# One block of a small transformer on one core: five q/k tiles in place of six, x loaded ahead of the weights, the first v product in three parts, and all engines' orders anew

## The chip, the cores and the metric

One Trainium2 chip, one core of it. The time is that of one execution of the whole kernel on the device, in microseconds (us); a kernel is compared by the median of several runs. The core has five engines that run their own instruction streams and wait for one another by semaphores: PE multiplies matrices, DVE and ACT do vector work and move results out of PE's accumulators (PSUM), POOL does small vector work, and SP issues the DMA transfers.

## The reference, cut to what matters

```python
x = A_x                                    # 2048 tokens x 448, bf16
h = x + A(layernorm(x), wqkv, wo)          # attention
out = h + B(layernorm(h), w_in, w_sp, b_sp, w_out)
# A: 16 heads of 28; token t sees t, t-2, ..., t-14; softmax over those 8; then @ wo
# B: z = gelu(h_n @ w_in); z1, z2 = halves of 896; z2 = layernorm(z2)
#    g = w_sp (2048x2048) @ z2 + b_sp; out = (z1 * g) @ w_out
```

## The kernel before, in words

Everything stays in on-chip memory; x is 16 blocks of 128 tokens. The work goes in these steps.

1. **Load.** SP issues 14 loads: x (16 blocks, in pieces of 1, 1, 2, 4, 4, 4), the q and k columns of `wqkv` (three parts into `wraw`, here wq_0, wq_1, wq_2 with 224, 448 and 224 KB), the v columns (two parts into `wv`, 224 KB each) and `wo` (three parts).
2. **Normalise.** For each block DVE takes statistics (L616, L618), POOL the inverse deviation (L610, L611), and DVE writes the normalised block `xn` (L627). Blocks 0 to 3 are transposed by PE (job xT, L656) and copied out of PSUM into `xhT` (job xe); blocks 4 to 15 are transposed by DMAs of SP.
3. **Weights.** DVE and ACT copy `wraw` into `wqk` with heads padded to 32 columns: jobs wp0 to wp3, k = 0 and 1 (336 columns each, need wq_0 and wq_1), and wp4_0, wp4_1 (448 columns, need wq_2).
4. **q and k.** For each tile of tokens in `QT` and each group of four heads one product of eight matmuls (L691 to L709): six full-height ones, "F", and two half-height ones, "H", that run side by side. Before there are six tiles, of 128, 128, 256 and three times 512 tokens. Job qk1_3H is the H part of tile 1, group 3; job qe evacuates the two PSUM banks into `qkT` on ACT or DVE. For tile 0 (`NF2 = 1`) the F part is two jobs, F0 and F1, that wait apart.
5. **v.** One product (job v0, v2, ..., v16, L715 to L731) for two of 18 attention blocks; six F and two H matmuls of 448 columns; job ve evacuates into `V1`.
6. **Attention.** For each block b: logits (jobs lg, two of 8 narrow matmuls each), exp on ACT (ex), mask on DVE (mk), E times V on PE (o), reciprocal and division on DVE (rc, om), a transposing DMA (oT). Then the output projection (y), residual and second layernorm.
7. **MLP.** Products with `w_in` (z1, z2), gelu on ACT, then 28 long products with `w_sp` (L950, job g) and the last ones with `w_out` (L974, job wo), residual add on DVE (L981, job r) and the store of each block.

The order on every engine isn't worked out when the kernel is built: `ORDER` lists all jobs by number in one sequence, each engine takes its own in that sequence, and `BANK` gives each product its PSUM banks. `ON` says which engine makes each evacuation or copy. A job waits for the jobs whose data or PSUM bank it needs; what stands behind it on the same engine waits with it. One filler job, "warm" (L989), is a matmul on constant data that may be listed many times; it stands there 32 times, 31 of them ahead of the first q and k product and one among the first ones.

Of the kernel before, what the change touches and what calls it, by code (L numbers as in the profile page):

```python
# [6 lines left out]
D = 448  # L7
# [6 lines left out]
NK = 128  # L14
# [11 lines left out]
ORDER = [1, 114, 23, 28, 5, 930, 930, 29, 4, 930, 930, 24, 930, 2, 930, 930, 3, 37, 25, 930, 39, 930, 6, 930, 930, 40, 930, 9,  # L26
# [41 lines left out]
BANK = [2, 1, 4, 5, 4, 6, 6, 0, 2, 0, 4, 2, 6, 0, 4, 6, 2, 4, 6, 2, 0, 4, 2, 0, 4, 2, 0, 0, 0, 2, 6, 1, 2, 0, 0, 2, 6, 4, 1,  # L68
# [9 lines left out]
ON = {'xe0_1': 'dve', 'xe0_0': 'dve', 'wp0_0': 'dve', 'wp2_1': 'dve', 'wp4_0': 'act', 'wp4_1': 'act', 'wp1_1': 'dve',  # L78
# [4 lines left out]
    'act', 've4': 'act', 'qe4_1': 'dve', 'od2': 'pool', 'od3': 'pool', 'qe4_3': 'dve', 've8': 'act', 'od4': 'pool',  # L83
    'qe4_0': 'dve', 'qe4_2': 'act', 've10': 'act', 'od6': 'dve', 'od5': 'pool', 'qe5_3': 'act', 'od7': 'pool', 'od8':
    'dve', 've12': 'act', 've14': 'act', 'qe5_1': 'act', 'qe5_0': 'act', 'od9': 'pool', 'od11': 'pool', 'od10':
    'pool', 'qe5_2': 'act', 'z2c1': 'act', 've16': 'act', 'z2c3': 'act', 'oc11': 'dve', 'z2c2': 'act', 'od12': 'pool',
    'oc12': 'act', 'od13': 'pool', 'z2c4': 'act', 'z2c5': 'act', 'z2c7': 'dve', 'z2c6': 'act', 'oc13': 'dve', 'od14':
    'dve', 'od15': 'pool', 'oc15': 'dve', 'od17': 'dve', 'oc14': 'dve', 'od16': 'pool', 'oc17': 'act', 'oc16': 'act',
    'z2c8': 'act', 'z2c9': 'act', 'z2c13': 'act', 'z2c10': 'act'}
RAW2 = [0, 1, 2, 1, 1, 1, 1, 2, 1, 2, 1, 0, 0, 1, 0, 0]  # L90
XEH = {0: 2}
# [9 lines left out]
FK = [(0, 2, 3), (0, 1, 3)]  # L101
# [218 lines left out]
def bass_sequential_preLN__sliding_local_dilated__mixer_gmlp__prompt_kernel(  # L320
# [17 lines left out]
    with contextlib.ExitStack() as top:  # L338
# [125 lines left out]
        def psv(t, k=0, n=512, p=128):  # L464
            c = (t.b + k) * 512
            return psum[0:p, c:c + n]
# [580 lines left out]
```

## Time and profile before

| | us |
|---|---|
| median of 3 runs | 242.99 (242.45 to 243.13) |
| the profiled execution's own time | 243.36 |
| its span in the trace | 241.6 |
| first q and k product starts on PE | 8.78 |
| the last add on DVE, behind PE's last matmul, starts | 239.08 |
| granted TensorE clock | 0.999 |

A row of a timeline gives the start, the time that the merged instructions took together, the engine, the line, the operation, the tiles, the shape and the count; in brackets the idle time ahead of it and what ended that. A row of the windows gives for one stretch of time the busy time of each engine with its number of instructions, the granted clock, the busy share of the DMA engines and the GB/s that they moved. "SPq" is SP's issuing of a DMA; "PEld" is PE's loading of weights. Some matmul records are missing from a trace: where one is, PE seems idle for the length of one matmul while its weight load is there.

### The profile page before, as it was taken

To read this page: it belongs to the slowest core of one execution; us is meant where nothing else is said; L and a number is where in the kernel's file an instruction comes from. 1 tells how busy PE (TensorE), PEld (TensorE's weight loads), DVE (VectorE), ACT (ScalarE), POOL (GpSimd) and SP (SyncE) were. 2 spreads that over 40 slices of the span, in tenths; PEclk is the share of its full clock that TensorE was granted. 3 is DMA by queue.
4 is the path that set the end of the run, shared out by engine and by line. 5 is a ranking of instruction groups with operands and counts; after the bars stand their busy time and mean duration, and the time that the engine had idled before them with its cause. 6 is when DMAs were issued, how large, how long until landed. Compare 5 with 4: busy or idle time off the path is not lost.

```text
span 241.6 us, 4270 instructions
## 1 busy us (share of the span) xinstructions
PE 234.5 (97%) x1742; PEld 115.9 (48%) x1759; DVE 148.9 (62%) x321; ACT 92.5 (38%) x116; POOL 33.3 (14%) x76
## 2 busy tenths in 40 slices
PE   7899999999999999999999999999999999999995
PEld 5665454554555554444444444444444444444443
DVE  4899987999886988798793143043109232245264
ACT  4687577884898887859440000000000000000000
POOL 6332202003250210131451000000000000000000
PEclk9999999999999999999999999999999999999999
DMA  6943354536749496889999990000000001100112
GB/s 171 341 120 69 65 109 97 133 87 158 164 87 132 90 136 126 174 137 180 188 199 209 187 171 0 3 0 0 0 3 19 19 1 49 49 0 0 38 60 76
DMA packets 66394, 23.23 MB, mean 96 GB/s; under 512 B 58694, under 2 KB 66246, under 8 KB 66374
## 3 DMA queue, kind: packets, MB, share of 16 engines
q1 hardware_dynamic: 66304, 22.95, 45.8%
q8 instruction: 14, 0.23, 0.4%
q14 instruction: 6, 0.05, 0.1%
q10 hardware_dynamic: 70, 0.00, 0.0%
HBM read 6.84 MB, written 1.84 MB: 36 GB/s over the span
## 4 chain that ended last, share of the span: by engine, by line
PE 92%; DVE 2%; DMA 2%; ACT 1%; SPq 1%; issue 1%; DVEq 0%
PE psum L950 40%; PE psum L498 38%; PE psum L974 9%; PE psum L789 3%; PE psum L813 3%; DMA wraw<-in_A_wqkv_dram 2%; DVE st L616 1%; SPq L529 1%; ACT V L514 0%; ACT E L798 0%; DVE wqk L514 0%; DVE xn L627 0%; DVE mv L618 0%; DVE srg L981 0%; DVE qkT L514 0%
## 5 line engine op out<-in xcount | busy, mean ns | idle before, releaser
L959 DVE TENSOR_TENSOR ub<-psum,bb 128x512 bf16<-128x512 f32 x28 | 19.2, 689 | 56.6 <-PE psum L950 56.1
L950 PE MATMUL psum<-wsp_hi,z2p 128*128 128x512 bf16 x219 | 49.9, 379 | 0.3
L798 ACT ACTIVATE E<-psum 128x896 bf16<-128x896 f32 (+2 forms) x36 | 31.7, 932 | 8.2 <-PE psum L789 8.2
L950 PEld LDWEIGHTS psum<-wsp_hi,z2p 128*128 128x128 bf16 x224 | 21.9, 98 | 26.0
L498 PE MATMUL psum<-xhT,wqk 128*128 128x512 bf16 (+5 forms) x186 | 27.3, 307 | 1.5 <-DVE wqk L514 0.5
L950 PE MATMUL psum<-wsp_lb,z2p 128*128 128x512 bf16 x109 | 25.5, 379 | 0.1
L950 PE MATMUL psum<-wsp_la,z2p 128*128 128x512 bf16 x109 | 25.0, 379 | 0.2
L498 PE MATMUL psum<-w_in,hnT 128*128 128x448 bf16 (+1 forms) x128 | 24.6, 353 | 0.0
L498 PE MATMUL psum<-hnT,w_in 128*128 128x512 bf16 (+1 forms) x112 | 23.8, 380 | 0.0
L974 PE MATMUL psum<-w_out,z1p 128*128 128x448 bf16 (+1 forms) x119 | 22.8, 341 | 0.0
L616 DVE BATCH_NORM_STATS2 st<-x_tm 128x6 f32<-128x448 bf16 x32 | 18.8, 612 | 1.8 <-DMA x_tm<-in_A_x_dram 1.7
L804 DVE TENSOR_TENSOR E<-E,maskb 128x1792 bf16<-128x1792 bf16 (+2 forms) x18 | 19.4, 1092 | 0.7 <-ACT E L798 0.7
L876 DVE BATCH_NORM_STATS2 st<-z2p 128x6 f32<-128x448 bf16 x32 | 18.5, 607 | 1.7 <-ACT z2p L872 1.1
L498 PEld LDWEIGHTS psum<-xhT,wqk 128*128 128x128 bf16 (+1 forms) x192 | 12.7, 97 | 12.9 <-issue 4.1
L981 DVE TENSOR_TENSOR srg<-psum,x_tm 128x448 bf16<-128x448 f32 (+1 forms) x17 | 9.9, 594 | 13.3 <-PE psum L974 7.8
L950 PEld LDWEIGHTS psum<-wsp_la,z2p 128*128 128x128 bf16 x112 | 10.9, 98 | 13.2
L950 PEld LDWEIGHTS psum<-wsp_lb,z2p 128*128 128x128 bf16 x112 | 11.0, 98 | 13.2
L611 POOL TENSOR_TENSOR rs<-rs,negh 128x2 f32<-128x2 f32 (+2 forms) x22 | 16.9, 770 | 1.8
L610 POOL TENSOR_SCALAR rs<-mv 128x2 f32<-128x2 f32 (+2 forms) x22 | 7.7, 352 | 66.3 <-DVE mv L618 47.1
L974 PEld LDWEIGHTS psum<-w_out,z1p 128*128 128x128 bf16 x119 | 11.6, 98 | 10.3
L498 PEld LDWEIGHTS psum<-w_in,hnT 128*128 128x128 bf16 (+1 forms) x128 | 10.4, 97 | 11.8 <-issue 3.0
L917 ACT ACTIVATE z1p<-psum 128x1024 bf16<-128x1024 f32 x14 | 14.1, 1021 | 4.5 <-PE psum L498 4.5
(53 smaller groups left out, 228.6 us busy)
## 6 DMA issues: line engine op xcount, KB each, us to landing
w_in<-in_B_w_in_dram SPq DMA_DIRECT2D x8, 224.0 KB, 3.2
out_dram<-srg SPq DMA_DIRECT2D x16, 112.0 KB, 1.8
x_tm<-in_A_x_dram SPq DMA_DIRECT2D x3, 448.0 KB, 7.1
w_out<-in_B_w_out_dram SPq DMA_DIRECT2D x1, 784.0 KB, 5.6
bb<-in_B_b_sp_dram SPq DMA_DIRECT2D x1, 512.0 KB, 5.2
wraw<-in_A_wqkv_dram SPq DMA_DIRECT2D x2, 224.0 KB, 2.9
wraw<-in_A_wqkv_dram SPq DMA_DIRECT2D x1, 448.0 KB, 5.7
wv<-in_A_wqkv_dram SPq DMA_DIRECT2D x2, 224.0 KB, 6.9
```

Source lines behind the costliest of these rows:

```text
L498: ins = e.matmul(o, w, x, start=g not in seen, stop=left[g] == 0, **kw)
L610: [(lambda e: e.tensor_single_scalar(A, mv[:, m:m + n, 1], EPS, ALU.add), r_mv[k][m:m + n], [rr]), (lambda e: e.tensor_tensor(R, A, negh[: ...
L611: (lambda e: e.tensor_tensor(R, A, negh[:, 0:1].to_broadcast([128, n]), ALU.pow), [rr, r_negh], r_rs[k][m:m + n])],
L616: [(lambda e: e.bn_stats(st[:, m, :], src), [rsrc], [r_st[k][m]])], dve_t(D))
L798: return e.activation(o, i, AF.Exp, scale=SCALE)
L804: return e.tensor_tensor(a, a, maskb[:, 0:1, pad:pad + nq].to_broadcast([NK, NHEAD, nq]), ALU.mult)
L876: [(lambda e, m=m, k=k: e.bn_stats(st3[:, m, k, :], z2p[:, m, D * k:D * (k + 1)]), [r_z2[m]], [r_st[2][m]])], dve_t(D))
L917: return e.activation(o, i, AF.Gelu_apprx_tanh)
L950: ins = e.matmul(psv(tk), z2p[:, s, 128 * fc:128 * fc + 128], w[:, 512 * (tc % 2):512 * (tc % 2) + 512], start=(s == 0), stop=(s == NB - 1))
L959: [(lambda e, tc=tc, s=s, tk=tk: e.tensor_tensor(ub[:, s, :], psv(tk), bb[:, 512 * tc:512 * tc + 512], ALU.add), [r_bb], [r_ub[s]])], dve_ ...
L974: ins = e.matmul(psv(tk, 0, c1 - c0), z1p[:, fc, 128 * m:128 * m + 128], w_out[:, fc, c0:c1], start=(fc == 0), stop=(fc == FC7 - 1))
L981: [(lambda e, m=m, s=s, tk=tk, c0=c0, c1=c1: e.tensor_tensor(srg[:, s, c0:c1], psv(tk, 0, c1 - c0), x_tm[:, m, c0:c1], ALU.add), [r_x[m]], ...
```

## The change

- `QT` has five tiles: 256, 256 and three times 512 tokens. So 64 matmuls of 128 columns become 32 of 256, eight evacuations of 256 columns become four of 512, and there are four products and four evacuations less. Tile 0, whose F part is in two jobs, now has 256 tokens and needs blocks 0 and 1 of x.
- `FIRST` and `ORDER` change the order of the loads. Before: x0, x1, wq_2, wq_0, wq_1, x2 (blocks 2 and 3), x4 (4 to 7), x12, wo_1, wv_0, wv_1, x8, wo_2, wo_0. After: x0, x1, x2, x4, wq_1, wq_0, wq_2, x8, wo_1, wv_0, wo_0, x12, wo_2, wv_1.
- The F part of v0 is two jobs, one for each attention block, with waits of their own; each waits for both parts of `wv` and for its own blocks of x. The other v products stay as they are.
- `ORDER`, `BANK` and `ON` are new throughout. PE begins with 22 warm matmuls, xT0, 7 warm, xT1, 3 warm, xT2, xT3, then all eight products of the first two tiles (512 tokens), then v0F0 v0F1 v0H v2H lg3_1 lg0_1 v2F v4F lg1_1 lg0_0 v4H and tile 2 (from qk2_2H on). Before it was xT0 and xT1, the products of the two 128-token tiles, xT2, the logits of block 0, xT3, v0, the 256-token tile with the logits of block 1 among it, v2, the logits of block 2, o1, o0, and then the first 512-token tile (from qk3_3F on). The jobs ve2, ve4 and ve8 go from ACT to DVE, and of the evacuations of 512-token tiles three are on DVE and not five.
- At the end PE did wo12, wo13, wo14 and last the two halves of wo15 (224 columns each); now it does both halves of wo15 first, then wo10, wo13, wo12 and last wo14 (448 columns).

```diff
-FIRST = [(0, 1), "q", (1, 2), (2, 4), "v", (4, 8), (8, 12), (12, 16), "o"]
+FIRST = [(0, 1), (1, 2), "v", "q", (2, 4), (4, 8), (8, 12), (12, 16), "o"]
-QT = [(0, 128), (128, 256), (256, 512), (512, 1024), (1024, 1536), (1536, 2048)]
+QT = [(0, 256), (256, 512), (512, 1024), (1024, 1536), (1536, 2048)]
...
-                load_c("wv", wv, A_wqkv[:, 2 * D:3 * D], D, W_v, 0.9, parts=[(None, 0, 2, 0), (None, 2, 2, 192)])
+                load_c("wv", wv, A_wqkv[:, 2 * D:3 * D], D, W_v, 1.05, parts=[(None, 0, 2, 0), (None, 2, 2, 192)])
...
-                return (
-                    [(i, psv(tk, i, D), xhT[:, c, k0:k0 + NK], wv[:, c, :], None) for i, k0 in enumerate(k0s) for c in FK[i]],
-                    [(i, psv(tk, i, D), xhT[p0:p0 + 64, c, k0:k0 + NK], wv[p0:p0 + 64, c, :], (p0, 0))
-                     for i, (k0, (c, p0)) in enumerate(zip(k0s, HK))])
+                fs = [[(i, psv(tk, i, D), xhT[:, c, k0:k0 + NK], wv[:, c, :], None) for c in FK[i]] for i, k0 in enumerate(k0s)]
+                hs = [(i, psv(tk, i, D), xhT[p0:p0 + 64, c, k0:k0 + NK], wv[p0:p0 + 64, c, :], (p0, 0))
+                      for i, (k0, (c, p0)) in enumerate(zip(k0s, HK))]
+                return fs + [hs] if b == 0 else [sum(fs, []), hs]
...
-            product("v%d" % b, key, f, W_v + xh_res(lo, hi), D, 3 * nb, tk, [o_jobs.get(b + i - NV) for i in range(nb)])
+            rd = W_v + xh_res(lo, hi)
+            if b == 0:
+                rd = [W_v + xh_res(k0, k0 + NK) for k0 in k0s]
+            product("v%d" % b, key, f, rd, D, 3 * nb, tk, [o_jobs.get(b + i - NV) for i in range(nb)], hreads=W_v + xh_res(lo, hi))
```

`ORDER` (962 entries before, 951 after), `BANK` and `ON` are lists of numbers and names, and left out here; what they do to the parts named above is told in the list.

More of the change, by code (lines that the diff above doesn't have):

```diff
@@ L25 @@
 LOOK = {'pe': 0.009410205530073946, 'act': 1e-09, 'dve': 0.19498114580727732, 'pool': 1e-09, 'sp': 0.13408016923274957}
-ORDER = [1, 114, 23, 28, 5, 930, 930, 29, 4, 930, 930, 24, 930, 2, 930, 930, 3, 37, 25, 930, 39, 930, 6, 930, 930, 40, 930, 9,
[41 rows of a table removed]
-BANK = [2, 1, 4, 5, 4, 6, 6, 0, 2, 0, 4, 2, 6, 0, 4, 6, 2, 4, 6, 2, 0, 4, 2, 0, 4, 2, 0, 0, 0, 2, 6, 1, 2, 0, 0, 2, 6, 4, 1,
[4 rows of a table removed]
+ORDER = [1, 27, 23, 25, 38, 2, 919, 28, 919, 8, 919, 29, 919, 919, 9, 37, 919, 24, 919, 6, 919, 114, 39, 919, 919, 5, 919, 40,
[40 rows of a table added]
+BANK = [2, 1, 4, 5, 2, 6, 0, 2, 0, 4, 6, 4, 6, 4, 6, 0, 2, 4, 4, 6, 0, 6, 0, 2, 0, 2, 2, 0, 2, 4, 1, 6, 2, 4, 0, 4, 4, 4, 1,
[4 rows of a table added]
 KEY = dict(x=-10.145, xs=0.685, qk=-3.702, qkg=-1.064, v=-1.761, ve=-6.148, qe=-3.15, lg=-1.488, ex=5.497,
@@ L77 @@
 WINB = 2
-ON = {'xe0_1': 'dve', 'xe0_0': 'dve', 'wp0_0': 'dve', 'wp2_1': 'dve', 'wp4_0': 'act', 'wp4_1': 'act', 'wp1_1': 'dve',
[4 rows of a table removed]
[L83 to L89, printed above, removed]
+ON = {'xe0_0': 'act', 'xe1_0': 'act', 'wp3_0': 'act', 'wp2_0': 'act', 'xe0_1': 'dve', 'wp1_0': 'dve', 'wp2_1': 'dve',
[3 rows of a table added]
+    'act', 'qe3_3': 'dve', 'od0': 'pool', 'od1': 'pool', 'qe2_1': 'act', 've6': 'act', 'qe3_0': 'dve', 'od3': 'pool',
+    'od2': 'pool', 'qe3_2': 'act', 've8': 'dve', 'od4': 'dve', 'od6': 'pool', 'qe3_1': 'act', 'qe4_1': 'act', 'qe4_0':
+    'act', 'od5': 'pool', 'qe4_2': 'act', 'qe4_3': 'act', 've10': 'act', 'od7': 'dve', 'od8': 'dve', 'od9': 'dve',
+    've14': 'act', 've16': 'act', 've12': 'act', 'od11': 'pool', 'od10': 'pool', 'oc11': 'dve', 'z2c1': 'act', 'z2c3':
+    'act', 'z2c2': 'dve', 'od12': 'pool', 'od13': 'pool', 'oc12': 'act', 'oc13': 'act', 'od15': 'dve', 'od14': 'pool',
+    'z2c4': 'act', 'od17': 'pool', 'oc14': 'act', 'oc15': 'act', 'od16': 'dve', 'oc17': 'dve', 'z2c6': 'act', 'z2c7':
+    'act', 'z2c5': 'act', 'oc16': 'dve', 'z2c9': 'act', 'z2c8': 'act', 'z2c10': 'act', 'z2c13': 'act'}
 RAW2 = [0, 1, 2, 1, 1, 1, 1, 2, 1, 2, 1, 0, 0, 1, 0, 0]
```

96 rows, old and new, of tables (BANK, ON, ORDER) are left out of this document.

## The prediction

> **What bounds the kernel now.** I read the page first, then the chain of waits in order of time, then the windows of its stages.
>
> ```profile
> span 241.6 us, 4270 instructions
> ...
> PE 234.5 (97%) x1742; PEld 115.9 (48%) x1759; DVE 148.9 (62%) x321; ACT 92.5 (38%) x116; POOL 33.3 (14%) x76
> ```
>
> ```profile
> 2.67 5.68 DMA wraw<-in_A_wqkv_dram
> ...
> 8.45 0.80 DVE wqk L514 x4
> ...
> 87.20 33.95 PE psum L498 x182
> ...
> 239.08 0.39 DVE srg L981
> ```
>
> ```profile
> core 0: us, PE busy (x) PEld busy (x) DVE busy (x) ACT busy (x) POOL busy (x), PEclk, DMA share, GB/s
> 2.00:8.00 6.00, 5.46 (x37) 4.07 (x36) 3.42 (x8) 2.41 (x5) 3.96 (x13) 1.00 0.90 258
> 8.00:13.00 5.00, 4.52 (x82) 3.61 (x84) 4.55 (x14) 3.91 (x11) 0.95 (x2) 1.00 1.09 366
> 8.78:22.38 13.60, 13.04 (x201) 8.94 (x201) 13.48 (x36) 11.65 (x22) 3.08 (x7) 1.00 0.60 175
> 22.38:87.20 64.82, 63.97 (x765) 32.56 (x772) 57.16 (x116) 50.20 (x59) 13.66 (x26) 1.00 0.56 109
> 87.20:121.20 34.00, 33.95 (x183) 14.70 (x182) 27.96 (x72) 24.88 (x30) 7.80 (x17) 1.00 0.88 162
> 121.20:239.08 117.88, 117.32 (x556) 55.26 (x565) 45.69 (x90) 2.45 (x3) 3.63 (x7) 1.00 0.26 52
> ```
>
> The kernel has three parts. Until 8.78 us it waits for q and k's weights: wq_1 lands at 2.67 + 5.68 = 8.35, the copies into `wqk` begin at 8.45. From 22.38 to 239.08 PE is full (63.97 of 64.82, 33.95 of 34.00, 117.32 of 117.88; most of what is left are missing records). In between, 8.78 to 22.38, PE and DVE are both all but full, and what follows the last matmul is one DVE instruction and a store. So the time is: when PE's first product starts, plus PE's work, plus PE's waits, plus the tail. The change keeps every product after the first 512 tokens; only these four can move.
>
> **Part 1, the start.** These rows give durations and landings.
>
> ```profile
> 1.51 4.55 PE L989 MATMUL psum<-warm 128*128 128x256 bf16 x21 [1.51 <-DVE warm L585]
> ...
> 2.87 0.63 DVE L616 BATCH_NORM_STATS2 st<-x_tm 128x6 f32<-128x448 bf16 x1 [1.42 <-DMA x_tm<-in_A_x_dram]
> 3.15 1.53 SPq L529 DMA_DIRECT2D x_tm<-in_A_x_dram  x3
> ...
> 7.05 1.25 PE L989 MATMUL psum<-warm 128*128 128x256 bf16 x10
> ...
> 8.43 1.23 ACT L514 ACTIVATE wqk<-wraw 128x336 bf16<-128x336 bf16 x3 [0.59 <-DMA wraw<-in_A_wqkv_dram]
> ...
> 9.31 3.39 PE L498 MATMUL psum<-xhT,wqk 128*128 128x128 bf16 x58
> ...
> 10.44 1.65 DVE L616 BATCH_NORM_STATS2 st<-x_tm 128x6 f32<-128x448 bf16 x3
> ...
> 12.54 0.39 PE L656 MATMUL psum<-ident,xn 128*128 128x128 bf16 x4
> 12.85 0.42 PE L789 MATMUL psum<-qkT 28*128 28x128 bf16 x16
> 13.18 0.37 DVE L618 BATCH_NORM_AGGREGATE mv<-st 128x2 f32<-128x6 f32 x4
> 13.77 1.28 DVE L514 CAST xhT<-psum 128x512 bf16<-128x512 f32 x2
> 13.91 1.60 PE L498 MATMUL psum<-wv,xhT 128*128 128x448 bf16 x8 [0.30 <-DVE qkT L514]
> 15.10 0.73 DVE L627 TENSOR_SCALAR xn<-x_tm,mv,rs 128x512 bf16<-128x512 bf16 x2
> 15.35 1.14 PE L498 MATMUL psum<-xhT,wqk 64*128 64x256 bf16 x10
> 15.54 5.22 SPq L528 DMA_TRANSPOSE xhT<-xn  x4
> 18.68 1.57 ACT L514 ACTIVATE qkT<-psum 128x512 bf16<-128x512 f32 x3
> ```
>
> ```profile
> x_tm<-in_A_x_dram SPq DMA_DIRECT2D x1, 224.0 KB, 5.8
> ...
> wo<-in_A_wo_dram SPq DMA_DIRECT2D x1, 336.0 KB, 7.7
> ...
> xhT<-xn SPq DMA_TRANSPOSE x12, 2.5
> ```
>
> Loads land in the order of issue. Up to wq_1 SP had issued 1120 KB, landed at 8.35; the next, x2's 224 KB, issued at 3.15, landed 5.8 later, at 8.95: 0.6 for 224 KB, as the 366 GB/s of the second window say. After the change wq_1 stands behind 896 KB of x, so it is complete with byte 1344 KB, wq_0 with 1568 KB, wq_2 with 1792 KB: 8.95, 9.55, 10.15. The bounds: by 8.00 the engines had moved 6 x 258 = 1548 KB in all, so if all ran level wq_0 lands at 8.1; if the wq parts are as slow behind x as they were in front, 10.2. I take 9.55.
>
> DVE has a chain of its own before the first copy now: six statistics (1.65 / 3 = 0.55), four aggregates (0.1 to 0.18), four normalisations (0.36), one half evacuation (0.4): 5.7 from 2.87, and some 0.7 of waits for x1, x2 and x4 to land, 9.3. Weights and DVE come out together; with 0.1 until the copy starts and 0.3 for it the first product starts at 9.95, not 8.78: **1.17 later**. Bounds 9.5 (DVE) and 10.6 (late weights).
>
> **Part 2, PE from there to the first 512-token tile.** Slots: 0.056 at 128 columns (58 in 3.39, the last with 0.2 of fill), 0.11 at 256 (two side-by-side pairs and six in 1.14), 0.19 at 448 (six and a pair in 1.60 with a change from full to half height, which costs 0.1). A product is seven slots. After: eight products, 56 x 0.11 = 6.2; four changes of height, 0.4; two waits, for wp3_1 and wp4_1 (ACT's copies take 1.23 / 3 = 0.41 each, one after another) and for a bank that qe0_1 frees, 0.2: PE comes to v0 at 16.75. Then v0, v2, v4, 21 x 0.19 = 4.0, four logits jobs at 0.2, five changes, 0.5: 22.05. ACT keeps up (ve0 ends at 19.3, ahead of v4 at 20.0). DVE frees v2's banks at some 22.15; I take 22.15 for the start of tile 2.
>
> ```profile
> 21.27 0.96 PE L813 MATMUL psum<-V,E 128*128 128x29 bf16 x32
> ...
> 22.38 0.99 PEld L498 LDWEIGHTS psum<-xhT,wqk 128*128 128x128 bf16 x6 [0.25 <-issue]
> ```
>
> Before, the same tile began at 22.38. By then PE had also done lg2 (0.4) and o0, o1 (0.9), by 22.15 after the change it has done v4 (1.33) instead: equal. So the opening **gains 0.23**. What pays for the 1.17: xT2 and xT3 are done before the weights come (0.4), the old waits go (13.60 - 13.04 = 0.56 of idle PE, some 0.8 with the fill of matmuls that counts as busy), six changes of height less (0.6), fewer small slots (0.1); less 0.3 of new waits. This list, coarser than the count, leaves 0.4; I keep the count.
>
> Two things sit close. xT4 to xT7 must land by then: after its first weight copy DVE has another, xe2 (0.64), the two wider copies (0.3 each), five statistics, four aggregates and n0_4, 5.0 in all, and so ends n0_4 at 15.2, against 15.10 + 0.4 before; the four transposes take 5.22 of SP and land 2.5 after issue, the last at 21.8 to 22.2. The loads ahead of them on SP are the same fourteen, so it isn't held longer. And v0 waits for wv_1, now the last load; the last load before (wo_0, issued 9.2) landed 7.7 later, at 16.9, against PE's 16.75. A wait of up to 0.3 is possible there; I take 0. The split of v0 by block is worth nothing: both parts wait for the same `wv`, and all of their x is there since xT1.
>
> **Part 3, the middle.** From tile 2 on the same matmuls follow in another order, with one change of height more (0.1). The old order had no wait there. The new one gives DVE three v evacuations and takes two of 512-token q/k tiles away:
>
> ```profile
> L514 ACT ACTIVATE V<-psum 128x896 bf16<-128x896 f32 x9 | 8.2, 920 | 5.4 <-PE psum L498 5.3
> ...
> L514 DVE CAST qkT<-psum 128x1024 bf16<-128x1024 f32 x5 | 6.1, 1216 | 0.4 <-PE psum L498 0.4
> ...
> L514 DVE CAST z2p<-psum 128x896 bf16<-128x896 f32 x1 | 1.1, 1083 | 0.0
> ```
>
> 3 x 1.08 - 2 x 1.22 = 0.8 us more for DVE, which has 57.16 of 64.82 busy. The cover is those 7.6 us; it is thinnest at o1, where DVE between 22.2 and mk1's end has ve4, qe2_2, two masks and small work, about 6.1, and PE about 6.4 of products ahead of o1. I put the middle's waits at 0.2 (from 0 to 1.5).
>
> **Part 4, the tail.** The last group is now 448 wide:
>
> ```profile
> L981 DVE TENSOR_TENSOR srg<-psum,x_tm 128x448 bf16<-128x448 f32 x15 | 9.1, 621 | 13.0 <-PE psum L974 7.5 <-DMA out_dram<-srg 5.5
> ...
> L981 DVE TENSOR_TENSOR srg<-psum,x_tm 128x224 bf16<-128x224 f32 x2 | 0.8, 391 | 0.3 <-PE psum L974 0.3
> ```
>
> 0.62 - 0.39 = **0.23 later**; matmul columns and the store are the same.
>
> **Sum**, against the profiled execution's 243.36: - 0.23 + 0.23 + 0.2 = 243.56. That execution lies 0.37 above the median of the runs, 242.99, so I forecast 243.2 for the median: nearly no change. Its own range is 242.3 to 243.7.
>
> **Rivals.** (a) *DVE takes over in the middle*: if it is more than 0.4 late at mk1, o1 waits, and as PE is full after that, nothing is caught up. With its 0.8 more and a last transpose 0.3 late that is 0.7 at o1 and as much again where ve8 stands ahead of rc6 and om6: 1.2 to 1.4, so 244.3. For it: DVE is busy 13.48 of 13.60 in the opening; against it: the 7.6 idle. (b) *The weights come as if all DMA engines ran level*: start at 9.5, no waits on copies or in the middle: 0.45 + 0.2 + 0.2 less, 242.35; with the waits of xT gone, 242.2. Against it: wq_1 landed at 8.35 although 1548 KB had been moved by 8.00. (c) *PE goes cold before the first product.* The 21 first warm matmuls took 0.21 each, the ten at 7.05 took 0.11: PE begins at half speed and needed some 4 us. After the change only 10 warm and 16 transposing matmuls stand between 6.3 and 9.95. If that is too thin, some 4 us of products run at half speed, 2 us: 245.2. Against it: PE was about as idle from 6.2 to 8.78 (waits of 0.5 and 0.7), and its 58 first products ran at 0.056. The Trainium skill (TensorE: Matmul & The Clock Gate, Part 1: The HAM clock gate) says that the clock is halved again after an idle window of about 3.4 us; no gap here is that long, so by that rule (c) doesn't happen, and the trace agrees as far as its gaps go. (d) *The change does not do what it says* for v0, as told: no time by itself, up to 0.3 if wv_1 is late, inside the forecast.
>
> **Chances.** Forecast with (d) 47%, (a) 31%, (b) 16%, (c) 6%. A measurement of this kernel tells about 0.3% (0.73 us) from no change. So faster 0.17, same 0.47, slower 0.36. Eight times in ten the time lies in 242.2 to 244.7: that takes in (b) and (a) and leaves out (c) and the far ends of the waits.
>
> **What would show it.** Right: the first L498 matmul at 9.5 to 10.6 after wraw's landing, no L656 work after it; tile 2's first weight load near 22.15; windows from there to 121 with under 0.5 us of idle PE beyond missing records; a last L981 of 0.62. Wrong: PE waiting for `wv` or `xhT` DMAs near 17 or 22, rows L813 or L498 with idle time ended by DVE between 25 and 60, matmuls of 256 columns at 0.21 after the start, or a first product before 9.3.

## The result and the profile after

| | before | after |
|---|---|---|
| median of the runs, us | 242.84 (12 runs) | 242.01 (12 runs, 241.32 to 242.84) |
| ratio | 1 | 0.9969 (0.9957 to 0.9981) |
| the profiled execution's own time | 243.36 | 242.38 |
| first q and k product | 8.78 | 9.99 |
| tile 2, first weight load | 22.38 | 21.70 |
| last add on DVE starts | 239.08 | 237.86 |
| its duration | 0.39 | 0.62 |

The kernel became 0.83 us faster (0.3%), where no change was forecast; against the profiled execution the sum said 243.56, and it is 242.38. One execution of a run told below ("after, exchanged and wo15 last") took 479.76 us for a reason that no trace shows; its ratio leaves it out, and the other five lie between 240.44 and 241.14. The page after has the same shares of busy time as before:

```profile
span 240.7 us, 4205 instructions
...
PE 233.6 (97%) x1711; PEld 114.9 (48%) x1727; DVE 148.9 (62%) x319; ACT 93.6 (39%) x115; POOL 32.3 (13%) x75
```

Next the windows, over the stretches that the prediction used:

```profile
core 0: us, PE busy (x) PEld busy (x) DVE busy (x) ACT busy (x) POOL busy (x), PEclk, DMA share, GB/s
...
8.78:22.38 13.60, 12.54 (x127) 8.02 (x128) 12.03 (x38) 10.54 (x19) 3.52 (x8) 1.00 0.62 171
22.38:87.20 64.82, 64.23 (x807) 32.90 (x812) 57.10 (x108) 54.04 (x64) 12.50 (x24) 1.00 0.56 109
87.20:121.20 34.00, 33.95 (x185) 14.77 (x185) 27.94 (x69) 26.10 (x30) 6.60 (x14) 1.00 0.76 137
```

PE is as full from 22.38 on as it was (64.23 of 64.82 against 63.97). In the opening DVE, which had 13.48 of 13.60, now has 12.03. The chain of waits gives the start, and the timeline the way from there to tile 2 (start, length, engine; in brackets the idle time ahead and what ended it):

```profile
3.26 6.37 DMA wraw<-in_A_wqkv_dram
...
9.65 0.29 DVE wqk L512
...
9.99 8.37 PE psum L496 x74
...
237.86 0.62 DVE srg L982
```

```profile
9.65 0.45 DVE L512 COPY wqk<-wraw 128x336 bf16<-128x336 bf16 x2 [0.69 <-DMA wraw<-in_A_wqkv_dram]
...
9.99 6.75 PE L496 MATMUL psum<-xhT,wqk 128*128 128x256 bf16 x64 [0.90 <-DVE wqk L512]
...
16.58 1.78 PE L496 MATMUL psum<-wv,xhT 128*128 128x448 bf16 x10
...
18.29 0.59 PE L790 MATMUL psum<-qkT 28*128 28x112 bf16 x16
...
18.82 2.44 PE L496 MATMUL psum<-wv,xhT 128*128 128x448 bf16 x12
...
20.16 1.09 DVE L512 CAST V<-psum 128x896 bf16<-128x896 f32 x1 [0.30 <-PE psum L496]
...
21.70 0.13 PEld L496 LDWEIGHTS psum<-xhT,wqk 64*128 64x128 bf16 x2
...
22.29 1.24 PE L496 MATMUL psum<-xhT,wqk 128*128 128x512 bf16 x5 [0.16 <-issue]
```

No row of PE between 9.99 and 21.70 has idle time ahead of it: the waits that the prediction put there (0.2 for copies and a bank, 0.1 for DVE) did not come. The landing of q and k's weights still sets the start, as before.

Where the 0.98 us of the profiled execution comes from, by the prediction's own marks: the start is 9.99 - 8.78 = 1.21 later; from there to tile 2 it takes 11.71 and not 13.60, 1.89 less; from tile 2 to the last add 237.86 - 21.70 = 216.16 and not 216.70, 0.54 less; the last add is 0.23 longer. Together 0.99 less.

### The profile page after: what moved, and what is told of

It reads as the page before. It is cut to its first block, busy times and chain, and to the rows that moved or that the text cites. A ratio compares the mean times of both kernels' runs of the same rounds, so it can differ in the third digit from the quotient of the medians.

```text
span 240.7 us, 4205 instructions
## 1 busy us (share of the span) xinstructions
PE 233.6 (97%) x1711; PEld 114.9 (48%) x1727; DVE 148.9 (62%) x319; ACT 93.6 (39%) x115; POOL 32.3 (13%) x75
## 4 chain that ended last, share of the span: by engine, by line
PE 93%; DMA 3%; DVE 1%; SPq 1%; issue 1%
PE psum L496 39%; PE psum L951 39%; PE psum L975 9%; PE psum L814 3%; PE psum L790 3%; DMA wraw<-in_A_wqkv_dram 3%; SPq L527 1%; DVE ub L960 1%; DVE z1p L963 0%; DVE srg L982 0%; DVE wqk L512 0%
## 5 line engine op out<-in xcount | busy, mean ns | idle before, releaser
L496 PE MATMUL psum<-xhT,wqk 128*128 128x512 bf16 (+3 forms) x154 | 26.5, 335 | 1.7 <-DVE wqk L512 0.9
L614 DVE BATCH_NORM_STATS2 st<-x_tm 128x6 f32<-128x448 bf16 x32 | 19.3, 613 | 2.0 <-DMA x_tm<-in_A_x_dram 2.0
L496 PEld LDWEIGHTS psum<-xhT,wqk 128*128 128x128 bf16 (+1 forms) x160 | 12.1, 97 | 11.7 <-issue 2.8
L512 ACT ACTIVATE qkT<-psum 128x1024 bf16<-128x1024 f32 (+1 forms) x17 | 13.6, 825 | 3.3 <-PE psum L496 3.0
L496 PEld LDWEIGHTS psum<-hnT,w_in 128*128 128x128 bf16 (+1 forms) x112 | 8.9, 97 | 12.2 <-issue 2.8
```

The costliest lines, as they stand in the source:

```text
L496: ins = e.matmul(o, w, x, start=g not in seen, stop=left[g] == 0, **kw)
L512: j = pl.job(name, eng, key, [(lambda e: e.activation(o(), i(), AF.Copy) if eng == "act" else e.tensor_copy(o(), i()), list(reads), list(w ...
L614: [(lambda e: e.bn_stats(st[:, m, :], src), [rsrc], [r_st[k][m]])], dve_t(D))
```

## The experiments

Every run is told by its ratio to the kernel before on the same chip (whose medians there were 242.6 to 242.9), and its profiled execution by three stretches. In the expectations P is the theory that time follows PE's own list of work, and T that other engines or waits set it. The mark in the table is the first full-height matmul of tile 2, because every profile shows it; it lies 0.25 after the weight load named above in the kernel before, and 0.59 after it in the changed kernel, which begins tile 2 with a half-height pair.

| kernel | median, ratio | first product | from it to the mark | mark to last add | last add |
|---|---|---|---|---|---|
| before | 242.84, 1 | 8.78 | 13.85 | 216.45 | 0.39 |
| before, loads of x first | 244.18, 1.0052 | 9.53 | 13.78 | 216.45 | 0.39 |
| before, five tiles | 244.84, 1.0076 | 8.24 | 16.45 | 216.45 | 0.39 |
| before, logits jobs exchanged | 242.01, 0.997 | 8.51 | 13.75 | 215.65 | 0.39 |
| after | 242.01, 0.9969 | 9.99 | 12.30 | 215.57 | 0.62 |
| after, once more | 241.5, 0.9948 | 9.64 | 12.31 | 215.75 | 0.62 |
| after, v0 in one piece | 242.1, 0.9969 | 10.23 | 12.31 | 215.51 | 0.62 |
| after, logits jobs exchanged | 240.93, 0.9931 | 9.12 | 12.09 | 215.15 | 0.62 |
| after, wo15 last | 241.64, 0.9968 | 9.81 | 12.39 | 215.54 | 0.39 |
| after, weights ahead of x4 | 241.46, 0.9952 | 8.83 | 12.61 | 215.56 | 0.62 |
| after, exchanged and wo15 last | 241.08, 0.9925 | 9.39 | 12.16 | 215.25 | 0.39 |
| after, all three edits | 241.04, 0.9928 | 8.98 | 12.62 | 215.15 | 0.39 |

### The middle: pairs of logits jobs

From tile 2 on the changed kernel runs nearly the same matmuls in another order and needs 0.54 less. (Ahead of tile 2 it now has v4; behind it, one pair of logits jobs more, o0 and o1.) In the chain of waits, each row of 16 narrow matmuls is two logits jobs next to each other on PE. Before:

```profile
32.41 0.33 PE psum L789 x16
...
34.86 0.50 PE psum L789 x16
...
40.54 0.50 PE psum L789 x16
...
47.71 0.50 PE psum L789 x16
...
51.64 0.51 PE psum L789 x16
...
64.76 0.51 PE psum L789 x16
...
72.99 0.67 PE psum L789 x16
...
76.03 0.51 PE psum L789 x16
```

After:

```profile
18.36 0.52 PE psum L790 x16
...
23.53 0.50 PE psum L790 x16
...
25.97 0.33 PE psum L790 x16
...
27.70 0.79 PE psum L814 x32
...
42.11 0.50 PE psum L790 x16
...
44.36 0.50 PE psum L790 x16
...
50.55 0.45 PE psum L790 x15
...
68.03 0.51 PE psum L790 x16
...
73.86 0.51 PE psum L790 x16
```

Nearly every pair takes either 0.33 or 0.50. (The row of L814 is o0 and o1.) A logits job j works on partitions 64j and 64j + 32 of `qkT`, with `tile_position` to match, so jobs of unlike j use different halves of PE's rows. The lists show that the pairs of 0.50 are those of like j (at 34.86 lg5_1 and lg6_1), the others those of unlike j. From tile 2 on there are six pairs of like j before and five after. The row of 0.67 before has unlike j (lg17_1 and lg16_0) and holds a wait: the timeline of the kernel before shows the eight weight loads of the second job 0.36 after the first eight.

```profile
72.92 0.21 PEld L789 LDWEIGHTS psum<-qkT 28*128 28x128 bf16 x8 [0.37 <-ACT E L798]
72.92 0.73 PE L789 MATMUL psum<-qkT 28*128 28x114 bf16 x16
...
73.28 0.21 PEld L789 LDWEIGHTS psum<-qkT 28*128 28x128 bf16 x8
```

So 0.34 for that wait and 0.17 for one pair make 0.51. The new order gives some of it back at 50.55, where lg9_0 and lg9_1, of unlike j, take 0.45 and not 0.33 because the second job starts late (the pair's weight loads are spread over 0.36 us, against 0.24 for the pair at 47.56): 0.12. That leaves some 0.4 of the 0.54. The rest is work that was moved: v4's seven slots of 0.19 come to 1.3, and a pair of logits jobs and o0 with o1 took 0.33 and 0.79 (25.97 and 27.70), so 0.1 to 0.2 less work is left behind tile 2. If the price of the pairs is right, exchanging the jobs j = 0 and 1 of a few blocks, with their exponentials and banks, takes 0.17 off each pair.

```diff
 # changed kernel, order on PE (blocks 3, 8, 14, 16 exchanged)
-lg3_1 lg0_1 ... lg3_0 lg1_0 ... lg8_0 lg5_0 ... lg7_1 lg8_1 ... lg14_1 lg17_1 ... lg17_0 lg16_0
+lg3_0 lg0_1 ... lg3_1 lg1_0 ... lg8_1 lg5_0 ... lg7_1 lg8_0 ... lg14_0 lg17_1 ... lg17_0 lg16_1
```

> The changed kernel, with the two logits jobs of blocks 3, 8, 14 and 16 (and their exps and banks) in exchanged places, so that none of the six pairs of logits jobs that use the same half of PE's rows stand next to one another. Theory P (PE is full from its first product to its last, so the time is the length of PE's own list): in the changed kernel a pair on the same half takes 0.36 us from first to last matmul and one on both halves 0.19, so six pairs give 6 x 0.17 = 1.0 us; about 241.0 against 242.0 for the changed kernel, ratio to the kernel before 0.993. Rival D (DVE, ACT and the transposes pace the middle, PE's list only fits into it): PE waits for exps and masks instead; the time stays at 241.8 to 242.2, ratio 0.996 to 0.998, and idle PE appears between 22 and 87 us.

```diff
 # kernel before, order on PE (blocks 6, 10, 15 exchanged)
-lg5_1 lg6_1 ... lg7_0 lg6_0 ... lg8_0 lg10_0 ... lg10_1 lg11_1 ... lg15_1 lg13_1 ... lg17_0 lg15_0
+lg5_1 lg6_0 ... lg7_0 lg6_1 ... lg8_0 lg10_1 ... lg10_0 lg11_1 ... lg15_0 lg13_1 ... lg17_0 lg15_1
```

> The kernel before, with the logits jobs of blocks 6, 10 and 15 in exchanged places, which parts all of its seven same-half pairs. Theory P: six pairs of 0.36 and one of 0.53 become 0.19: 1.0 to 1.3 us less, 241.5 to 241.9 against 242.84, ratio 0.995. Rival D: no change, ratio 0.999 to 1.001. If this holds and the same in the changed kernel does too, the logits' order is one part of what the new order won.

Measured: 240.93 (4 runs), ratio 0.9931 (0.9916 to 0.9946) for the changed kernel, and 242.01 (6 runs), 0.997 (0.9958 to 0.9982) for the kernel before. In the changed kernel five of the six exchanged pairs behave as P says. Three of them in its chain (the rows at 18.36, 23.53 and 68.03 are now these):

```profile
17.46 0.35 PE psum L791 x16
...
22.45 0.33 PE psum L791 x16
...
66.88 0.33 PE psum L791 x16
```

The sums are smaller than the count of pairs. In the changed kernel five pairs should give 0.85 behind the mark, and 0.42 went, with another 0.21 ahead of it. What is missing is lost at two places, which the timeline of PE shows. The pair of lg8_1 and lg5_0, at 40.80, is of unlike j now, but the next product begins 0.49 after the pair's first matmul, as it did without the exchange (42.05 to 42.54): the second job starts late (the pair's weight loads take 0.35), and nothing is won. And at 46.69 PE, now earlier, waits 0.24 for a transposed output.

```profile
40.80 0.51 PE L791 MATMUL psum<-qkT 28*128 28x112 bf16 x16
41.29 1.29 PE L497 MATMUL psum<-wo,OT 128*128 128x448 bf16 x6
...
46.69 1.59 PE L497 MATMUL psum<-wo,OT 128*128 128x448 bf16 x8 [0.24 <-DMA OT<-otm]
```

In the kernel before six pairs should give 1.0, and from the mark to the last add 0.80 went. Here 0.16 is lost at one place, behind lg15_0 and lg13_1: the pair is 0.18 shorter, but the product behind it now has idle time ahead of it and had none. The row of 0.67 that the expectation counts as a seventh pair of like j is not one, and it stayed at 0.67. The median fell by 0.6 and not by 1.0 to 1.3, so P's size is a miss there, though its sign is right and D's "no change" is ruled out.

```profile
64.25 1.59 PE L499 MATMUL psum<-w_in,hnT 128*128 128x448 bf16 x8 [0.16 <-issue]
```

The median of 240.93 was a hit for a reason that is only in part P's: the profiled execution also began its products at 9.12, not 9.99 (see the scatter below).

### The start: the loads

Do the loads alone cost what the prediction says, or does the earlier x pay at once?

```diff
 # kernel before, order of the loads
-x0 x1 wq_2 wq_0 wq_1 x2 x4 ...
+x0 x1 x2 x4 wq_2 wq_0 wq_1 ...
```

> The kernel before with x's first eight blocks loaded ahead of q and k's weights, nothing else changed. P: the weights land 1.0 to 1.3 us later, the first product moves from 8.5 to 8.8 to about 9.6 to 10.0, and as PE is full from tile 2 on the end moves by as much: ratio 1.004 (1.002 to 1.006). T (the opening is set by ACT and DVE, which the earlier x serves better): the start is as late, but the stretch from first product to tile 2 shrinks by more than 0.5 from 13.60, ratio 1.000 to 1.002.

Measured: 244.18 (4 runs), ratio 1.0052 (1.0037 to 1.0067). The timeline of this kernel has the first product and the first full-height one of tile 2 at

```profile
9.53 0.52 PE L499 MATMUL psum<-xhT,wqk 128*128 128x128 bf16 x6 [1.51 <-DVE wqk L515]
...
23.31 1.78 PE L499 MATMUL psum<-xhT,wqk 128*128 128x512 bf16 x9 [0.32 <-issue]
```

so the opening is as long as it was (13.78 against 13.85), and the rest has the same 216.45: the loads alone are a plain loss. Next the opposite edit, in the changed kernel: the weights ahead of x4, and the statistics of two late blocks moved behind DVE's weight copies.

```diff
 # changed kernel, order of the loads
-x0 x1 x2 x4 wq_1 wq_0 wq_2 x8 ...
+x0 x1 x2 wq_1 wq_0 wq_2 x4 x8 ...
```

> The changed kernel, with q and k's weights issued ahead of blocks 4 to 7 of x (and the statistics of blocks 4 and 6 on DVE behind the weight copies). The first product then starts near 8.8 us instead of 9.99. Theory P alone (start plus PE's list): 1.2 us less, 240.8, ratio 0.992. Theory T (the four transposes of blocks 4 to 7, one after another on SP and landing at 21.64 in the changed kernel, are next in line, since x's blocks 4 to 7 land later): tile 2 still begins near 21.7, PE waits about 1 us for it, and the time stays within 0.3 us of the changed kernel's 242.0, ratio 0.996 to 0.998.

Measured: 241.46 (4 runs), ratio 0.9952 (0.9939 to 0.9965). The first product comes at 8.83, 1.16 sooner, and at tile 2 part of that is lost to the blocks of x that now come late (timeline of this kernel):

```profile
20.86 0.12 PEld L497 LDWEIGHTS psum<-xhT,wqk 64*128 64x128 bf16 x2 [0.42 <-DVE xn L626]
...
20.89 0.39 PE L497 MATMUL psum<-xhT,wqk 64*128 64x512 bf16 x2 [0.18 <-DVE xn L626]
```

Both theories hold in part: in these two profiles x4 first costs 1.16 at the start and saves 0.3 at tile 2. The ratio, 0.9952, can't be told from the changed kernel's (0.9969, and 0.9948 when it ran once more, below).

### The opening: tiles and split

```diff
 # kernel before: tiles alone; the products of the second 128-token tile leave the order
-QT = [(0, 128), (128, 256), (256, 512), ...
+QT = [(0, 256), (256, 512), ...
```

> The kernel before with one part of the change alone: five tiles of q and k, the first of 256 tokens, in place of six; loads and the order of the rest stay. P (time follows PE's own list; the second tile of 128 tokens cost its own weight loads, which 128-column products don't cover): first product at 8.5 to 8.8 as before, tile 2 starts 0.1 to 0.5 us sooner after it than the 13.60 us of before, ratio 0.998 (0.996 to 1.000). T (in the opening ACT and DVE set the time, with the copies of the v product and the exponentials before tile 2): the stretch stays within 0.1 of 13.60, ratio 1.000. If this run alone gives the 1.9 us by which the opening shrank in the changed kernel, the tiles were the whole of it; below 0.5, most came from the order.

Measured: 244.84 (4 runs), ratio 1.0076 (1.0047 to 1.0105): a miss for both. P's reason isn't in the rows of the kernel before either: 58 products of 128 columns ran at 0.056 us each, half of the 0.11 at 256, so their weight loads did not show. The timeline of PE shows waits for evacuations that the old order and banks put in the way, and the windows what followed:

```profile
12.20 1.04 PE L487 MATMUL psum<-xhT,wqk 64*128 64x256 bf16 x8 [1.18 <-ACT qkT L503]
...
13.93 0.47 PE L778 MATMUL psum<-qkT 28*128 28x128 bf16 x16 [0.47 <-ACT qkT L503]
```

```profile
13.50:14.00 0.50, 0.07 (x6) 0.07 (x9) 0.50 (x1) 0.37 (x1) 0.50 (x1) 1.00 0.17 57
14.00:14.50 0.50, 0.50 (x18) 0.35 (x19) 0.19 (x1) 0.03 (x1) 0.40 (x2) 0.69 0.01 2
14.50:15.00 0.50, 0.50 (x5) 0.38 (x4) 0.02 (x1) 0.50 (x1) 0.31 (x2) 0.50 0.00 0
...
17.50:18.00 0.50, 0.50 (x8) 0.26 (x5) 0.50 (x2) 0.29 (x1) 0.00 (x0) 0.90 1.22 168
```

(The number behind POOL's is the granted clock.) From 14.2 to 17.6 the clock was 0.50. That is the half speed that rival (c) speaks of, in another kernel and behind other waits; of the four executions two had a mean clock of 0.99 and 245.4 us, two about 1.00 and 244.1 to 244.3. So five tiles in the old order lose some 1.4 us at full clock, which the rows put down to the waits, and some 1.2 more when the clock falls. Only an execution of the second kind was profiled.

The split of v0 undone:

```diff
 # changed kernel, order on PE
-v0F0 v0F1 v0H
+v0F v0H
```

> The changed kernel with the first v product made in one piece again (it waits for both blocks of wv's and x's parts at once). P: the parts are all there before PE reaches it, so no change: ratio to the kernel before 0.997 (0.995 to 0.998), the stretch from first product to tile 2 is 11.7 as in the changed kernel. T (the split hides a late part of wv, whose last load lands at 15.2 and is copied after that): 0.2 to 0.5 us later, ratio 0.998 to 0.999, with an idle time of PE ahead of the first 448-column product.

Measured: 242.1 (10 runs), ratio 0.9969 (0.9953 to 0.9984), with the opening at 12.31 as in the changed kernel: the split is worth nothing.

### The tail, and what adds up

```diff
 # changed kernel, order on PE at the end
-wo15_0 wo15_0#1 wo10_0 ... wo13_0 wo12_0 wo14_0
+wo10_0 ... wo13_0 wo12_0 wo14_0 wo15_0 wo15_0#1
```

> The changed kernel, with the two halves of the last block's output product, their adds and the store moved to the end, as in the kernel before. Theory P and the prediction's tail: the last add takes 0.39 instead of 0.62, so 0.23 us less, about 241.8, ratio 0.996. Rival: the last store or another wait hides it and the time stays at 242.0, ratio 0.997.

Measured: 241.64 (12 runs), ratio 0.9968 (0.9949 to 0.9986). The profile has the 0.23 that the prediction charged to the tail; its last instruction is

```profile
237.74 0.39 DVE L983 TENSOR_TENSOR srg<-psum,x_tm 128x224 bf16<-128x224 f32 x1 [0.28 <-PE psum L976]
```

and the time up to its start (215.54) has not changed. The ratio can't tell 0.23 us, 0.1%, from the changed kernel's 0.9969. Then the three edits together, logits jobs, loads and tail:

> The changed kernel with three edits together: the two logits jobs of blocks 3, 8, 14, 16 exchanged, q and k's weights loaded ahead of x's second four blocks, the last wo product and its residual at the end. P (the gains lie in different stretches and add up): from the single runs 0.6 in the pairs, 0.3 at the tail and 0.6 to 0.8 at the start below 242.0, so 240.4 (240.0 to 240.8), ratio 0.991. T (one gain is taken by a wait of another: the sooner start already waited 0.35 for a transposed block of x at tile 2, and PE running ahead waited 0.24 for a transposed output): 240.9, ratio 0.993, no better than the exchange alone.

Measured: 241.04 (4 runs), ratio 0.9928 (0.9909 to 0.9948), what T expects: the start is sooner (8.98), and tile 2 waits 0.36 for the normalised x ahead of its first matmul, so the mark stands at 21.60, no sooner than 21.21 in the run of the exchange alone. To see what the start is worth, the changed kernel ran once more, and the exchange with the tail but without the new loads:

> The changed kernel itself, unedited, once more. Of four profiled executions with its list of loads three began the first product at 9.8 to 10.2 and one, that of the exchanged logits jobs, at 9.12. P (the landing of q and k's weights scatters from one execution to the next, whatever the program): spans of the single executions lie over a width of about 1 us, from 239.9 to 241.0, the stretch from first product to tile 2 in this profile is 11.7 again, and from tile 2 to the last instruction's start 216.2. T (the start is fixed for a program): first product at 9.9 to 10.0, spans within 0.4 of 240.7.

> The changed kernel with the logits jobs of blocks 3, 8, 14, 16 exchanged and the last wo product and its residual at the end; the loads as in the changed kernel. P: from tile 2 to the last instruction's start 215.6 and 0.39 after it, so 0.6 and 0.23 less than the changed kernel: 241.1 if the weights land as they mostly do, 240.6 if they land as in the run with the exchange alone; ratio 0.992 (0.990 to 0.994). T (the 240.93 of the exchange alone was owed to early landings in its four executions): 241.3 or more, ratio 0.994 or above.

Measured: 241.5 (6 runs, spans 239.4 to 240.5), ratio 0.9948 (0.9927 to 0.9969), with the first product at 9.64 and the later stretches as in the first profile to 0.2; and 241.08 (6 runs), ratio 0.9925 (0.9906 to 0.9945). So one program's start scatters over a good part of a microsecond. The exchange with the tail is faster than the kernel before. Against the changed kernel it is ahead of 0.9969, but its interval overlaps that of 0.9948 on the same chip; and its ratio can't be told from that with the loads as well.

## Why the prediction was wrong

The forecast, 243.2, was 1.2 too high (242.01 lies just below its range of 242.2 to 244.7), and nearly all of the error stands in two terms.

1. **The start** was right: 9.99 for 9.95, released by the weights (0.69 of idle DVE ahead of its copy), not by DVE's own chain. The six executions with this list of loads lie from 9.12 to 10.23, 9.70 on the mean; three with the old list from 8.24 to 8.78, 8.51 on the mean, 1.19 sooner. That one execution came within 0.04 is luck, as single starts lie up to 1.1 apart. The loads alone in the old kernel cost about as much as predicted for them, 244.18.
2. **The opening was mis-sized**: the step "two waits ... 0.2", the slots to tile 2 (5.3) and "DVE frees v2's banks at some 22.15". Measured: PE reached v0 at 16.58, not 16.75, with no wait; it needed 21.70 - 16.58 = 5.12; and DVE ended v2's evacuation at 20.16 + 1.09 = 21.25, before PE was done with v4. From first product to tile 2 that is 11.71 and not 12.20: 0.49. The coarser list of gains beside the count, which the prediction put aside, left 0.4 against 0.23 and was nearer to the measured 0.68. DVE wasn't the bound there any more; it had 12.03 of 13.60. That the work done by tile 2 is equal held to 0.1 or 0.2.
3. **The middle was wrong in kind**: "From tile 2 on the same matmuls follow in another order", at the same price but 0.1 for a change of height (which its sum leaves out) and 0.2 of waits, and "The old order had no wait there". The old one had one: 0.34 at 72.99. The new one has no idle PE that ends on another engine, and 0.12 at a late second job, 50.55. And the same matmuls don't take the same time in another order: two logits jobs on one half of PE's rows take 0.50, on two halves 0.33, and the old order had one such pair more behind tile 2. That makes some 0.4 of the 0.54, and the work moved ahead of tile 2 the rest; with the 0.2 of waits put in the sum, the term was off by 0.74. What the exchanged jobs show is the price of a pair; that the wait at 72.99 went with the new order is read from the two traces and not tried by itself.
4. **The tail** was right: 0.62 for 0.39, and with the old end back 0.39.

The four differences, +0.04, -0.49, -0.74 and 0, make the 1.18 by which 243.56 was above 242.38, to 0.01.

The rivals. (a) did not come: no idle time of PE behind tile 2 is ended by DVE, and DVE was busy there for no longer than before (57.10 for 57.16 from 22.38 to 87.20), as ve2 is done by then (20.16 to 21.25). DVE is close behind all the same: as PE ran ahead by some tenths in the exchange, a transposed output of DVE's came 0.24 late. (b) came nearest, with 242.2 to 242.35, and partly by luck: its waits that don't come are right, but the start was not at 9.5 but at 9.99. (c) did not come in this kernel; PE's matmuls of 256 columns ran at full clock from the first on (64 in 6.75). It came in the old order with five tiles, where no gap was longer than 1.18 and PE idled 1.7 of the 3.2 us ahead of the fall (1.18 and 0.47, the two rows above). The rule that the prediction weighed, a whole idle window, does not cover this; the Trainium skill (TensorE: Matmul & The Clock Gate, A second HAM failure mode: psum-queue depth-cycling) says that a PE which stops often and briefly between its groups can lose its clock too, and these rows, with two waits, agree as far as they go. (d) held: the split is worth nothing.

Is the gain of the opening one of the tiles, the loads or the order? Tiles alone lose 2.6 us there, loads alone give 0.07, the split nothing; only with the new order and its banks do 1.55 go (1.89 by the prediction's mark). How the 1.55 divides between fewer small matmuls, x that is ready before the first product, and banks that come free in time was not tried apart.

## What to carry to other kernels

An order written out by hand is part of the cost: before taking "the same matmuls in another order" at no price, list each group's time in the chain of waits by its neighbours. Here an exchange of a few jobs between their places, without any other change, took 0.63 off the profile (0.21 and 0.42), about as much as the opening gained net of its later start (1.89 - 1.21 = 0.68). In the kernel before, six exchanged jobs alone gave the ratio of the whole change, 0.997 against 0.9969. A start bought with loads is only worth what the next late operand leaves of it: 1.16 sooner became 0.85 in the profile here, and nothing in the run of all three edits, against one whose weights had landed early.

## What the runs showed of the hardware

- Packed narrow matmuls that follow on the same half of PE's rows take 0.50 us for 16, on both halves 0.33 where the two jobs start together. A second job that starts late makes it 0.45 (50.55) or 0.67 (72.99). The Trainium skill (TensorE: Matmul & The Clock Gate, Part 3: Packing small matmuls, The mechanism) has weight loads overlap with running matmuls only where the row groups differ; the windows of the two kinds of pair (weight loads of `qkT` alone) agree with that, as the weight loads are busy for 0.41 us in the one and 0.23 in the other, for 16 loads each.

```profile
core 0: us, PEld busy (x), PEclk, DMA share, GB/s
23.45:24.05 0.60, 0.41 (x16) 1.00 0.29 57
25.90:26.30 0.40, 0.23 (x16) 1.00 0.94 177
```

- The same loads, in the same order, let the first product begin at 9.12 in one execution and at 10.23 in another, while all that follows repeats to about 0.2. A difference of a few tenths between medians of few runs can come from there.
- In the old order with five tiles TensorE's clock fell to half for 3.4 us (14.2 to 17.6) after two waits of 1.18 and 0.47; two of four executions have a mean clock that shows it.
